# Attention and feed-forward on one core: score matmuls with 128 stationary columns, and reciprocal pieces moved behind each feed-forward step

## The chip, the cores and the metric

The kernel runs on one core of a Trainium2 chip. The metric is the time on the device in microseconds, as a median of several executions; before the change it is 482.2 us (481.5 to 483.6). A trace's span is some 1.8 us shorter than the time of the same execution. All executions told of here were fast ones, with a mean granted TensorE clock of 0.98 or more.

## The reference

```python
q, k, v: (8, 12, 448, 64) fp32;  w_gate, w_val: (768, 1536);  w_out: (1536, 768)
scores = (q @ k.T) / 8                       # per batch and head
attn = exp(scores - max) / (sum(exp(scores - max)) + 1e-9)
x = (attn @ v), heads side by side           # (8*448, 768)
g = x @ w_gate
out = (g * sigmoid(g) * (x @ w_val)) @ w_out # (3584, 768) fp32
```

The kernel leaves the maximum out (the scores are small) and divides by the sum after the product with v.

## The kernel before

Heads go in 48 pairs. For each pair the 448 keys are four chunks of P = 112. A chunk's scores come out keys by queries, so the keys are the stationary operand; the two heads of the pair lie in partitions 0 to 63 and 64 to 127, and their matmuls run side by side in two halves of the array's rows:

```python
def qk_half(pr, half):
    t = qkT[pr]                                    # [128, 2*NC, P]: Q chunks, then K chunks
    for c in (2 * half, 2 * half + 1):
        s = ps_s.tile([P, 2, 512], FP32, tag="s")
        for hx in range(2):
            nc.tensor.matmul(s[:, hx, 0:S],
                lhsT=t[ts(hx, 64), NC + c, :],     # 64 rows, 112 columns
                rhs=t[ts(hx, 64), 0:NC, :].rearrange("p c q -> p (c q)"), ...)
        nc.scalar.activation(E[pr][:, c], s[:, :, 0:S], AF.Exp, scale=sm_scale)
```

Every second pair, the sums of two pairs' exponentials are inverted in four pieces on VectorE, spread over the partitions by four transfers (Rb<-R, below "the broadcast"), and multiplied into X on GpSimd. This work goes into a list, and the feed-forward takes from it:

```python
def sums(p0):
    ...                                            # ssb <- acc, on VectorE
    for i in range(4):
        work.append(lambda i=i: nc.vector.reciprocal(R[:, ts(i, P)], ssb[:, ts(i, P)]))
    def bcast(): ...                               # nc.sync: four transfers R -> Rb
    work.append(bcast)
    return work, [mult(p0), mult(p0 + 1)]          # on GpSimd: X <- xr * Rb

def ffn_run(budget):
    while backlog and budget > 0:
        gen, t = backlog.pop(0)
        pop_deferred(2 if t < 1.5 else 4)          # ahead of the step
        next(gen)                                  # a gp step, a vp step or an op step
        ...
```

A gp step is six matmuls and sg = tanh on ScalarE; a vp step is six matmuls, then t = (sg + 1) * gp and hts = t * vp on VectorE; an op step is twelve matmuls and a copy to osb on ScalarE. gp, vp, op and the sums rotate through three PSUM buffers. osb has two buffers, each freed when its write to the output has landed. SyncE's queue carries, in order, the loads of q and k, the transposing transfers that make qkT from casts done on GpSimd (from pair 11 on, three pairs ahead), the broadcasts and the output writes.

The softmax here doesn't subtract the row's maximum and nothing guards it: scores larger than these inputs give would overflow.

Of the kernel before, what the change touches and what calls it, by code (L numbers as in the profile page):

```python
# [10 lines left out]
FP32 = mybir.dt.float32  # L11
FP16 = mybir.dt.float16
AF = mybir.ActivationFunctionType
# [12 lines left out]
def kernel(  # L26
# [10 lines left out]
    nc = tc.nc  # L37
    B, H, S, D = q.shape
    DM = H * D
    DF = moe_w_gate.shape[1]  # L40
    P = 112
    NC = S // P
# [6 lines left out]
    sm_scale = float(D) ** -0.5  # L49
# [19 lines left out]
    ps_s = ctx.enter_context(tc.tile_pool(name="ps_s", bufs=2, space=PSUM))  # L69
# [6 lines left out]
    ident = consts.tile([P, P], FP16, name="ident")  # L76
# [15 lines left out]
    raw = {}  # L92
    v16 = {}
    qkT = {}
    E = {}
# [48 lines left out]
    def prep(pr):  # L144
        rq, rk = raw[pr]
        if pr == 0 or pr >= NPE:
            qk16 = attp.tile([P, 2, NC, 2, D], FP16, tag="qk16", bufs=3)
            eng = nc.vector if pr == 0 else nc.gpsimd
            for t, src in enumerate((rq, rk)):
                eng.tensor_copy(qk16[:, t].rearrange("p c h d -> p h c d"), src[:])  # L150
        qkT[pr] = attp.tile([128, 2 * NC, P], FP16, tag="qkT", name="qkT", bufs=5)
        if pr >= NPE:
            nc.sync.dma_start_transpose(
                qkT[pr][:], qk16[:].rearrange("p t c h d -> p (t c h d)")
            )
            return None

        def turn():
            tp = ps_f.tile([128, 2 * NC, 128], FP16, tag="f", name="tp")
            for t in range(2):  # L160
                for c in range(NC):
                    for hx in range(2):
                        src = qk16[:, t, c, hx] if pr == 0 else raw[pr][t][:, hx, c, :]
                        nc.tensor.transpose(tp[ts(hx, 64), t * NC + c, 0:P], src, ident[:])  # L164
                if pr == 0 and t == 0:
                    nc.vector.tensor_copy(qkT[pr][:, 0:NC], tp[:, 0:NC, 0:P])
            lo = NC if pr == 0 else 0
            nc.vector.tensor_copy(qkT[pr][:, lo:], tp[:, lo:, 0:P])

        return turn  # L170

    def qk_half(pr, half):
        if half == 0:
            E[pr] = ep.tile([P, NC, 2, S], FP16, tag="E", name="E")
        t = qkT[pr]
        for c in (2 * half, 2 * half + 1):
            s = ps_s.tile([P, 2, 512], FP32, tag="s")
            for hx in range(2):
                nc.tensor.matmul(  # L179
                    s[:, hx, 0:S],  # L180
                    lhsT=t[ts(hx, 64), NC + c, :],
                    rhs=t[ts(hx, 64), 0:NC, :].rearrange("p c q -> p (c q)"),
                    start=True,
                    stop=True,
                )
            nc.scalar.activation(E[pr][:, c], s[:, :, 0:S], AF.Exp, scale=sm_scale)  # L186

    def pv(pr):
        g, r = divmod(pr, GP)
# [15 lines left out]
    def mult(pr, eng, rb, lo=0, hi=S):  # L205
        b, hp = divmod(pr, NHP)
        kk, bb = divmod(b, NB)
        if kk not in X:
            X[kk] = xp.tile([128, NCB, NB * S], FP16, tag="X", name="X")
        eng.tensor_tensor(  # L210
            X[kk][:, hp, bb * S + lo : bb * S + hi], xraw[pr][:, lo:hi], rb[:, lo:hi], ALU.mult
        )

    def sum_rows(p0, acc):
        for c in range(NC):
            for j in range(4):
                nc.tensor.matmul(  # L217
                    acc[ts(j, 32), 0:S],
                    lhsT=ones[:],
                    rhs=E[p0 + j // 2][:, c, j % 2, :],  # L220
                    start=(c == 0),
                    stop=(c == NC - 1),
                )
# [19 lines left out]
    def sums(p0):  # L243
        acc = ps_f.tile([128, 512], FP32, tag="f")
        sum_rows(p0, acc)
        ssb = attp.tile([128, S], FP32, tag="ssb", bufs=1)
        nc.vector.tensor_copy(ssb[:], acc[:, 0:S])  # L247
        R = attp.tile([128, S], FP32, tag="R", bufs=2)
        work = []
        for i in range(4):  # L250
            work.append(lambda i=i: nc.vector.reciprocal(R[:, ts(i, P)], ssb[:, ts(i, P)]))  # L251

        def bcast():
            for u in range(2):
                rb = attp.tile([128, S], FP32, tag="Rb", name="Rb")
                rv = rb[:].rearrange("(r two) s -> two r s", two=2)
                for w in range(2):
                    nc.sync.dma_start(rv[w], R[ts(u, 64), :])
                Rb[p0 + u] = rb

        work.append(bcast)
        return work, [lambda u=u: mult(p0 + u, nc.gpsimd, Rb[p0 + u]) for u in range(2)]

# [80 lines left out]
    with tc.manual_schedule():  # L344
# [17 lines left out]
        for _ in range(7):  # L362
            nc.tensor.matmul(wp[:], lhsT=warm[:, 0:128], rhs=warm[:], start=True, stop=True)
        prep(0)()
        turn = prep(1)

        wq = {
# [18 lines left out]
        deferred = []  # L386
# [5 lines left out]
        def pop_deferred(n=1):  # L392
            for _ in range(n):
                if deferred:
                    deferred.pop(0)()

        def add_block(i):
            f1, f2, n = block(i)
            t1, t2 = NCB * n / 2400.0, NFB * OH / 2400.0
            a = [(f1, t1)] * (2 * NFB)  # L400
            pend = list(ffn2_wait)
            ffn2_wait.clear()
            seq = []
            m = len(pend)
            done = 0
            for x in range(len(a)):
                seq.append(a[x])
                want = (x + 1) * m // len(a)
                while done < want:
                    seq.append(pend[done])  # L410
                    done += 1
            seq += pend[done:]
            own = [(f2, t2)] * (2 * (n // 128))
            if i == 0:
                seq += own
            else:
                ffn2_wait.extend(own)
            backlog.extend(seq)
            state["left"] += sum(t for _, t in seq)

        def ffn_run(budget):
            while backlog and budget > 0:
                gen, t = backlog.pop(0)
                pop_deferred(2 if t < 1.5 else 4)
                next(gen)
                budget -= t
                state["left"] -= t
            return budget

        carry = 0.0  # L430
# [4 lines left out]
        for pr in range(NPAIR + 1):  # L435
            if pr in add_at:
                pop_deferred(99)
# [8 lines left out]
            if pr < NPAIR:  # L446
                qk_half(pr, 0)
            if pr == 0:
                turn()
            if pr + 3 < NPAIR and pr + 3 >= NPE:  # L450
                prep(pr + 3)
# [7 lines left out]
            if pr > NHP and pr % 2 == 0:  # L459
                work, mults = sums(pr - 2)  # L460
                deferred.extend(work)
                held[pr + 1] = mults
            if pr in add_at:
                add_block(add_at[pr])
            for w in wq.pop(pr, []):
                emit(w)
            carry = ffn_run(state["left"] / slots + carry)
            if pr < NPAIR:
                qk_half(pr, 1)
# [8 lines left out]
            if not backlog:  # L478
                pop_deferred(7)
            carry = ffn_run(state["left"] / max(1, slots - 1) + carry)  # L480
        for fns in held.values():
            deferred.extend(fns)
        ffn_run(1e9)
        pop_deferred(99)
        add_block(B - 1)
# [33 lines left out]
```

## Time and profile before

| | before |
|---|---|
| time, median | 482.2 us |
| TensorE busy | 465.8 of 480.3 us |
| first gp step starts | at 40.0 us |
| first gp to the start of the last matmul | 435.9 us |
| TensorE waits for t in that stretch, between starts | 7, sum 5.8 us |

The first 40 us (warm-up, first loads, attention only) differ between executions, and TensorE runs its first matmuls at half clock for a varying time. What sets that is left open. So I compare, besides times, the stretch from the first gp to the start of the last matmul, and give TensorE's losses between starts: the distance of two starts less the streaming time, less 2.5 ns, and less 95 ns where the tiling changes.

The lines below, from the timeline before, give the first group of sums (start, duration, engine, line, operation):

```profile
50.03 2.99 DVE L251 RECIPROCAL R<-ssb 128x112 f32<-128x112 f32 x4
52.93 0.49 DVE L288 SCALAR_TENSOR_TENSOR t<-sg,gp 128x384 f32<-128x384 f32 x1
53.04 2.46 SPq L258 DMA_DIRECT2D Rb<-R  x4
53.48 1.14 PE L268 MATMUL gp<-X,wg 128*128 128x384 f16 x6 [1.08 <-DVE t L288]
```

Four pieces run together, t stands behind them, the next gp waits for t's buffer; and the broadcast leaves at 53.04.

### The profile page before, as it was taken

How to read it: one execution, taken by the hardware profiler on the slowest of the kernel's cores; microseconds unless marked ns; L12 is line 12 of the kernel's file. 1: busy time of each engine (PE TensorE's matmuls, PEld its weight loads, DVE VectorE, ACT ScalarE, POOL GpSimd, SP SyncE). 2: the span in 40 equal slices, each digit the busy share in tenths (PEclk: the TensorE clock that was granted, in tenths of full speed). 3: DMA queues.
4: the chain of work that ended last, by engine and by line, in shares of the span. 5: the costliest groups of instructions: out<-in, count | busy, mean ns of one | idle time of the engine just before them, and what ended most of it. 6: DMA issues, size and time to landing. Idle time of an engine off the chain costs nothing.

```text
span 480.3 us, 8813 instructions
## 1 busy us (share of the span) xinstructions
PE 465.8 (97%) x3559; PEld 226.1 (47%) x3559; DVE 242.1 (50%) x383; ACT 237.5 (49%) x345; POOL 120.7 (25%) x164
## 2 busy tenths in 40 slices
PE   8989999999999999999999999999999999999996
PEld 3435444434444555444444554444444445554553
DVE  3676775167764644636635536446365446343310
ACT  4765555655555455454555465454545551222221
POOL 8534023533243034024042140330320111000000
PEclk9999999999999999999999999999999999999999
DMA  9999999995784596636667476945532212101123
GB/s 138 195 209 239 196 226 182 273 202 125 125 172 97 130 178 140 148 83 162 123 122 179 98 135 131 190 106 129 121 77 65 59 40 72 51 16 33 34 66 100
DMA packets 86025, 62.03 MB, mean 129 GB/s; under 512 B 38496, under 2 KB 82528, under 8 KB 85984
## 3 DMA queue, kind: packets, MB, share of 16 engines
q1 hardware_dynamic: 63872, 46.53, 42.2%
q0 software_dynamic: 22048, 14.88, 22.6%
q8 instruction: 28, 0.46, 0.4%
q14 instruction: 13, 0.11, 0.1%
q10 hardware_dynamic: 64, 0.05, 0.0%
HBM read 47.19 MB, written 11.01 MB: 121 GB/s over the span
## 4 chain that ended last, share of the span: by engine, by line
PE 90%; DVE 6%; ACT 2%; DMA 1%; issue 0%; SPq 0%; ACTq 0%
PE op L304 23%; PE vp L280 22%; PE gp L268 21%; PE s L179 10%; PE acc L194 8%; DVE R L251 4%; PE acc L217 4%; ACT E L186 2%; PE tp L164 1%; PE rb L236 1%; DVE ssb L247 1%; DMA rk<-in_k_dram 1%; DVE t L288 1%; DMA out_dram<-osb 0%; ACT osb L319 0%
## 5 line engine op out<-in xcount | busy, mean ns | idle before, releaser
L186 ACT ACTIVATE E<-s 112x896 f16<-112x896 f32 x192 | 164.5, 915 | 34.0 <-PE s L179 33.9
L268 PE MATMUL gp<-X,wg 128*128 128x384 f16 (+1 forms) x576 | 125.1, 353 | 1.1 <-DVE t L288 1.1
L280 PE MATMUL vp<-X,wv 128*128 128x384 f16 (+1 forms) x576 | 124.9, 353 | 0.5 <-DVE t L288 0.5
L304 PE MATMUL op<-wo,hts 128*128 128x384 f16 x672 | 117.0, 326 | 3.4 <-DVE t L288 3.4
L210 POOL TENSOR_TENSOR X<-xr,Rb 128x448 f16<-128x448 f32 x42 | 47.5, 1133 | 264.6 <-DMA Rb<-R 182.7
L276 ACT ACTIVATE sg<-gp 128x384 f32<-128x384 f32 (+1 forms) x96 | 52.3, 545 | 105.7 <-PE gp L268 105.7
L288 DVE SCALAR_TENSOR_TENSOR t<-sg,gp 128x384 f32<-128x384 f32 (+1 forms) x96 | 58.3, 607 | 79.4 <-ACT sg L276 79.4
L304 PEld LDWEIGHTS <-hts 128*128 128x128 f16 x672 | 64.9, 98 | 51.9 <-issue 8.3
L268 PEld LDWEIGHTS <-wg 128*128 128x128 f16 x576 | 52.6, 98 | 60.8 <-issue 17.3
L280 PEld LDWEIGHTS <-wv 128*128 128x128 f16 x576 | 54.3, 98 | 57.2 <-issue 9.1
L202 DVE COPY xr<-acc 128x448 f32<-128x448 f32 x48 | 29.9, 623 | 92.0 <-PE acc L194 92.0
L291 DVE SCALAR_TENSOR_TENSOR hts<-t,vp 128x384 f16<-128x384 f32 (+1 forms) x96 | 59.6, 621 | 32.2 <-PE vp L280 24.8
L319 ACT ACTIVATE osb<-op 128x384 f32<-128x384 f32 x55 | 27.0, 490 | 97.2 <-PE op L304 93.0
L251 DVE RECIPROCAL R<-ssb 128x112 f32<-128x112 f32 x84 | 62.9, 810 | 0.7
L179 PE MATMUL s<-qkT 64*112 64x448 f16 x384 | 58.9, 378 | 3.8 <-ACT E L186 3.2
L194 PE MATMUL acc<-E,vt 112*32 112x448 f16 x768 | 45.9, 360 | 0.0
L179 PEld LDWEIGHTS <-qkT 64*112 64x112 f16 x384 | 18.6, 126 | 39.2 <-issue 36.3
L194 PEld LDWEIGHTS <-vt 112*32 112x32 f16 x768 | 16.2, 96 | 24.6 <-issue 16.8
L150 POOL CAST qk<-rk 112x512 f16<-112x512 f32 x37 | 22.7, 614 | 0.0
L150 POOL CAST qk<-rq 112x512 f16<-112x512 f32 x37 | 22.7, 613 | 0.0
L217 PE MATMUL acc<-E,ones 112*32 112x448 f16 x384 | 22.3, 353 | 0.0
L126 POOL DMA_DIRECT2D vt<-in_v_dram x17 | 13.5, 792 | 2.7 <-PE acc L194 2.4
(37 smaller groups left out, 94.6 us busy)
## 6 DMA issues: line engine op xcount, KB each, us to landing
Rb<-R SPq DMA_DIRECT2D x84, 112.0 KB, 2.3
rq<-in_q_dram SPq DMA_DIRECT2D x38, 224.0 KB, 3.8
rk<-in_k_dram SPq DMA_DIRECT2D x38, 224.0 KB, 4.0
vt<-in_v_dram POOLq DMA_DIRECT2D x15, 336.0 KB, 6.3
out_dram<-osb SPq DMA_DIRECT2D x7, 336.0 KB, 3.1
wg<-in_moe_w_gate_dram POOLq DMA_DIRECT2D x4, 576.0 KB, 17.8
wv<-in_moe_w_val_dram POOLq DMA_DIRECT2D x4, 576.0 KB, 19.6
wo<-in_moe_w_out_dram POOLq DMA_DIRECT2D x3, 768.0 KB, 28.5
```

Source lines behind the costliest of these rows:

```text
L150: eng.tensor_copy(qk16[:, t].rearrange("p c h d -> p h c d"), src[:])
L179: nc.tensor.matmul(s[:, hx, 0:S], lhsT=t[ts(hx, 64), NC + c, :], rhs=t[ts(hx, 64), 0:NC, :].rearrange("p c q -> p (c q)"), start=True, sto ...
L186: nc.scalar.activation(E[pr][:, c], s[:, :, 0:S], AF.Exp, scale=sm_scale)
L194: nc.tensor.matmul(acc[ts(j, 32), 0:S], lhsT=vt[:, 2 * r + j // 2, c, ts(j % 2, 32)], rhs=E[pr][:, c, j // 2, :], start=(c == 0), stop=(c ...
L210: eng.tensor_tensor(X[kk][:, hp, bb * S + lo : bb * S + hi], xraw[pr][:, lo:hi], rb[:, lo:hi], ALU.mult)
L251: work.append(lambda i=i: nc.vector.reciprocal(R[:, ts(i, P)], ssb[:, ts(i, P)]))
L268: nc.tensor.matmul(gp[:, 0:n], lhsT=wslice("g", fb, cb), rhs=X[kk][:, cb, ds(c0, n)], start=(cb == 0), stop=(cb == NCB - 1),)
L276: nc.scalar.activation(sg[:, 0:n], gp[:, 0:n], AF.Tanh, scale=0.5)
L280: nc.tensor.matmul(vp[:, 0:n], lhsT=wslice("v", fb, cb), rhs=X[kk][:, cb, ds(c0, n)], start=(cb == 0), stop=(cb == NCB - 1),)
L288: nc.vector.scalar_tensor_tensor(t1[:, 0:n], sg[:, 0:n], 1.0, gp[:, 0:n], ALU.add, ALU.mult)
L291: nc.vector.scalar_tensor_tensor(hts[:, fb, 0:n], t1[:, 0:n], 0.5 * HS, vp[:, 0:n], ALU.mult, ALU.mult)
L304: nc.tensor.matmul(op[:, 0:OH], lhsT=hts[:, fb, ts(ch, 128)], rhs=wo[fb // (NFB // 3)][:, fb % (NFB // 3), ts(oh, OH)], start=(fb == 0), s ...
```

## The change

The intent: give the score matmuls the full 128 stationary columns (the 16 beyond the chunk make rows of PSUM that nobody reads), and keep the reciprocals from standing in a row ahead of the feed-forward's own VectorE work.

```diff
-            s = ps_s.tile([P, 2, 512], FP32, tag="s")
+            s = ps_s.tile([128, 2, 512], FP32, tag="s")
...
-                    lhsT=t[ts(hx, 64), NC + c, :],
-                    rhs=t[ts(hx, 64), 0:NC, :].rearrange("p c q -> p (c q)"),
+                    lhsT=t[ts(hx, 64)].rearrange("p c q -> p (c q)")[:, c * P : c * P + 128],
+                    rhs=t[ts(hx, 64), NC:, :].rearrange("p c q -> p (c q)"),
...
-            nc.scalar.activation(E[pr][:, c], s[:, :, 0:S], AF.Exp, scale=sm_scale)
+            nc.scalar.activation(E[pr][:, c], s[0:P, :, 0:S], AF.Exp, scale=sm_scale)
...
+        bcast.light = True
         work.append(bcast)
...
             for _ in range(n):
                 if deferred:
                     deferred.pop(0)()
+                while deferred and getattr(deferred[0], "light", False):
+                    deferred.pop(0)()
...
-                pop_deferred(2 if t < 1.5 else 4)
                 next(gen)
                 budget -= t
                 state["left"] -= t
+                pop_deferred(1 if t < 1.5 else 2)
```

(Cut: the places that fill qkT are changed so that the K chunks come first; the last chunk's 16 extra columns then lie within the tile.)

More of the change, by code (lines that the diff above doesn't have):

```diff
@@ L149, in prep @@
             for t, src in enumerate((rq, rk)):
-                eng.tensor_copy(qk16[:, t].rearrange("p c h d -> p h c d"), src[:])
+                eng.tensor_copy(qk16[:, 1 - t].rearrange("p c h d -> p h c d"), src[:])
         qkT[pr] = attp.tile([128, 2 * NC, P], FP16, tag="qkT", name="qkT", bufs=5)
@@ L162, in turn @@
                     for hx in range(2):
-                        src = qk16[:, t, c, hx] if pr == 0 else raw[pr][t][:, hx, c, :]
-                        nc.tensor.transpose(tp[ts(hx, 64), t * NC + c, 0:P], src, ident[:])
+                        src = qk16[:, 1 - t, c, hx] if pr == 0 else raw[pr][t][:, hx, c, :]
+                        nc.tensor.transpose(tp[ts(hx, 64), (1 - t) * NC + c, 0:P], src, ident[:])
                 if pr == 0 and t == 0:
-                    nc.vector.tensor_copy(qkT[pr][:, 0:NC], tp[:, 0:NC, 0:P])
-            lo = NC if pr == 0 else 0
-            nc.vector.tensor_copy(qkT[pr][:, lo:], tp[:, lo:, 0:P])
+                    nc.vector.tensor_copy(qkT[pr][:, NC:], tp[:, NC:, 0:P])
+            hi = NC if pr == 0 else 2 * NC
+            nc.vector.tensor_copy(qkT[pr][:, 0:hi], tp[:, 0:hi, 0:P])
         return turn
```

## The prediction

> **What bounds the kernel now.** I read the page's busy shares first, then the chain that ended last, then the list of waits, then single stretches of the timeline. The page says:
>
> ```profile
> PE 465.8 (97%) x3559; PEld 226.1 (47%) x3559; DVE 242.1 (50%) x383; ACT 237.5 (49%) x345; POOL 120.7 (25%) x164
> ...
> PE 90%; DVE 6%; ACT 2%; DMA 1%; issue 0%; SPq 0%; ACTq 0%
> ```
>
> TensorE is the bound: 97% busy, 90% of the chain. The chain gives VectorE 6%, 4.4% of it (21 us) to the reciprocal line. That is not a possible gain: a chain walks back through whatever ran, and TensorE was mostly working meanwhile. What a VectorE change can give back is only what TensorE lost, so I take the list of waits, its TensorE rows alone:
>
> ```profile
> PE op L304 <- DVE t L288: 3.4, 5, 1.1
> ...
> PE s L179 <- ACT E L186: 3.2, 7, 0.9
> ...
> PE gp L268 <- DVE t L288: 1.1, 1, 1.1
> ...
> PE vp L280 <- DVE t L288: 0.5, 1, 0.5
> ```
>
> (Columns: microseconds in all, how often, the longest.) Seven waits, 5.0 us, are for the first VectorE instruction of a feed-forward step (t). The timeline shows where one comes from:
>
> ```profile
> 367.32 2.99 DVE L251 RECIPROCAL R<-ssb 128x112 f32<-128x112 f32 x4
> ...
> 367.73 0.49 ACT L276 ACTIVATE sg<-gp 128x384 f32<-128x384 f32 x1 [1.12 <-PE gp L268]
> ...
> 369.12 1.15 PE L268 MATMUL gp<-X,wg 128*128 128x384 f16 x6
> ...
> 370.23 0.49 DVE L288 SCALAR_TENSOR_TENSOR t<-sg,gp 128x384 f32<-128x384 f32 x1
> ...
> 370.78 2.11 PE L304 MATMUL op<-wo,hts 128*128 128x384 f16 x12 [0.51 <-DVE t L288]
> ```
>
> sg is ready at 368.2, but four reciprocal pieces stand ahead of t in VectorE's order and hold it from about 368.2 to 370.2. The feed-forward rotates through three PSUM buffers; gp and vp of this step and gp of the next hold them, so op stands until t has read the first gp.
>
> **The cost of a score set.** Scores come in sets of four matmuls, two row halves side by side, then two more. I looked at one set, and at the gp group that follows it:
>
> ```profile
> L179 PEld LDWEIGHTS <-qkT x4: 123/124/126, 189.8 to 189.8; 64*112 64x112 f16 x4
> L179 PE MATMUL s<-qkT x4: 349/371/393, 189.8 to 190.0; 64*112 64x448 f16 x4
> ```
>
> ```profile
> L268 PEld LDWEIGHTS <-wg x6: 95/98/98, 190.3 to 191.0; 128*128 128x128 f16 x6
> L268 PE MATMUL gp<-X,wg x6: 326/326/336, 190.3 to 191.1; 128*128 128x384 f16 x6
> ```
>
> (Durations are minimum/median/maximum in ns.) After a change of shape the weights cannot be loaded ahead: the first load and the first matmul start within 2 ns of each other in the records (189.827 and 189.829), so the matmul includes the load. For 112 columns that costs 393 - 349 = 44 ns over the second pair, whose load was hidden; for 128 full columns (gp) only 336 - 326 = 10 ns. The start distance confirms it: first to second pair 233 ns (189.829 to 190.062), against 448/2.4 = 187.
>
> **What the Trainium skill says.** "TensorE: Matmul & The Clock Gate", section "Weight-path perf modes — Fast Weight Load (FWL) and DoubleRow": the fast load is on when the number of weights is 128 and the type is not FP32. The trace agrees: loads of 128 columns have a median of 98 ns, those of 112 columns 123. "TensorEngine Tiling (Array Packing)", section "Restrictions", says that column tiling disables the fast load; row tiling, which the scores use, is not named. No run so far shows a 64-row load of 128 columns. The same page's "Key Properties" says that a change of tiling mode drains TensorE: here each switch costs about 95 ns (vp to s 256 ns between starts, against 160 of streaming; s to gp 282 against 187). The change leaves every switch. "Perfetto Trace Analysis", section "Summary: the profiler window per engine type", says that a matmul's end is estimated; so I count losses between starts.
>
> **The change part by part.** *Stationary columns 112 to 128.* Matmul count, moving columns (448) and exponentials are the same; sixteen more PSUM rows are written and not read, and TensorE's time goes by moving columns. K is put ahead of Q in the tile only so that the last chunk's 16 extra columns lie within it; both were needed by the first matmul anyway. The saving is 44 - 10 = 34 ns for each of 384/4 = 96 sets, 3.3 us. Some 8 sets in the first 40 us wait for ScalarE's exponentials, so there it is hidden: 88 x 34 = 3.0 us. If the two row halves load one after the other, the second adds another 10 ns: 88 x 24 = 2.1 us. I take 2.7.
>
> *Reciprocals.* The same 84 pieces, about 747 ns each (2.99/4), same VectorE sum. In the new instruction order the typical run is: one piece, t and hts, one or two pieces, t and hts, and the last one, in place of four ahead of t. For the stretch above: ssb copied at 367.3, one piece until 368.1, t from 368.2 (ready sg) to 368.7, hts when vp ends, then the rest. The first gp is free at 368.7 and op wants it at 370.1: 1.4 us to spare. Two pieces together (1.5 us) may delay the next t, but a wait of 0.5 to 1.1 us after four pieces means that with 1.5 us less nothing is left. Counted between starts, the seven losses beyond streaming and a switch's 95 ns are 1.15 (at 53.5 us), 0.67 (69.9), 0.68 (146.1), 0.69 (258.5), 0.68 (370.8), 0.67 (386.2), 1.30 (401.1): 5.8 us. It is more than 5.0 because the modelled matmul tail, 326 - 162 = 164 ns, hides part of a gap. After 40 us I find no other gap above 60 ns that is not a switch, so nothing stands behind these seven: 5.8 us come off.
>
> *The broadcast and the X products move later.* The broadcast now follows its last piece at once, but that piece lies 1 to 2 steps later; the products come out of the list one at a time. By the sum of streaming times in program order they move 1 to 3 us. The last product before a block's first gp ends, before and in order of blocks, 1.5, 6.2, 9.5, 10.1, 7.2, 8.4 and 10.3 us ahead of it (for the first: product done 94.3, gp 95.8). The tight first one lies in a stretch of op steps where VectorE has no feed-forward work, so its four pieces still run together and its broadcast keeps its place in the DMA queue. No wait should arise.
>
> Sum: 5.8 + 2.7 = 8.5 us; 482.0 - 8.5 = 473.5 us.
>
> **Rivals.** *The fast load doesn't engage with 64 rows.* Then the load grows by 16 columns, about 7 ns at one column per 2.4 GHz cycle (an estimate), 96 x 7 = 0.7 us lost, and 482.0 - 5.8 + 0.7 = 476.9. For it: no load of this form is in the trace; against: the rule as stated has no row condition. I give it one in six. *The products become the wait.* If the broadcasts stall the SP queue or products land late, blocks start late by 1 to 2 us each: 475 to 480. For it: the 1.5 us margin; against: the other margins of over 6 us. *VectorE as the new bound.* It is half busy, with runs of reciprocals moved rather than added; if half the seven waits came back elsewhere, 476.4. *The chain taken at its word:* 21 us of reciprocals would make 461; the TensorE waits speak against it.
>
> **Range and chances.** The reciprocal part is nearly sure, the weight part likely. Everything at its best (44 ns x 96 = 4.2 us, and 5.8) gives 472.0, just beyond the 2% line at 472.3. So the likely result is just within 2%. I say 473.5 us, 471.5 to 477.0; faster by over 2% 0.15, within 2% 0.83, slower 0.02.
>
> **What would show it.** Right: score loads near 98 ns and the first matmul of a set near 360 ns in place of 393; the three TensorE rows that wait for t gone; the gain of the weights spread evenly over 0 to 392 us, that of the reciprocals in steps at the seven places. Wrong: score loads at 123 ns or above; a TensorE wait for X; new waits for t after two or three pieces in a row. Most dangerous to the number is what I have not seen in the trace at all, the speed of the 64-row fast load.

## The result

The changed kernel takes 474.6 us (474.1 to 475.1, four executions), against 482.2 us. The ratio is 0.984, interval 0.981 to 0.987. The time lies in the range forecast, 1.1 us above the figure in it.

The page of the changed kernel, busy shares and chain:

```profile
PE 461.7 (98%) x3559; PEld 219.4 (46%) x3559; DVE 245.3 (52%) x383; ACT 237.4 (50%) x345; POOL 120.8 (26%) x164
...
PE 91%; ACT 3%; DMA 3%; issue 1%; SPq 0%; DVE 0%; POOL 0%; ACTq 0%; POOLq 0%
```

VectorE has gone from the chain (6% to 0%), yet the time fell by 1.6%: its share in the chain was no measure of the gain. DMA went from 1% to 3% and ScalarE from 2% to 3%.

The list of waits after. No TensorE row waits for t any more; these have grown or are new:

```profile
PE s L179 <- ACT E L186: 4.4, 10, 0.9
...
ACT osb L320 <- DMA out_dram<-osb: 3.0, 1, 3.0
...
PEld L179 <- DMA qkT<-qk: 0.9, 1, 0.9
```

Before, the first was 3.2 us in 7 waits, the second 1.5 us, and the third did not exist.

The score line by itself, over the whole trace after (minimum/median/maximum in ns):

```profile
L179 PEld LDWEIGHTS <-qkT x384: 92/93/115, 6.1 to 385.9; 64*128 64x128 f16 x192
L179 PE MATMUL s<-qkT x384: 346/359/578, 6.1 to 386.1; 64*128 64x448 f16 x192
```

The load fell from 123 to 93 ns, the first matmul of a set from 393 to 359; the second pair has a median of 349 in both traces.

The stretch of the timeline that answers to the one in the prediction (the same step, 4.2 us earlier):

```profile
363.11 0.85 DVE L251 RECIPROCAL R<-ssb 128x112 f32<-128x112 f32 x1
...
363.52 0.49 ACT L277 ACTIVATE sg<-gp 128x384 f32<-128x384 f32 x1 [1.09 <-PE gp L269]
364.04 0.56 DVE L289 SCALAR_TENSOR_TENSOR t<-sg,gp 128x384 f32<-128x384 f32 x1
...
365.18 2.27 DVE L251 RECIPROCAL R<-ssb 128x112 f32<-128x112 f32 x3
365.86 1.30 PE L305 MATMUL op<-wo,hts 128*128 128x384 f16 x7
```

One piece, then t as soon as sg is there, and op starts with no wait; three pieces run after hts, where nobody needs VectorE.

Between 74 and 94 us, though, TensorE now waits where it did not. The timeline there:

```profile
59.44 8.26 SPq L153 DMA_TRANSPOSE qkT<-qk  x1
...
70.31 4.16 SPq L153 DMA_TRANSPOSE qkT<-qk  x1
...
74.56 2.46 SPq L258 DMA_DIRECT2D Rb<-R  x4
...
76.75 0.11 PEld L179 LDWEIGHTS <-qkT 64*128 64x128 f16 x4 [0.90 <-DMA qkT<-qk]
76.76 0.55 PE L179 MATMUL s<-qkT 64*128 64x448 f16 x4 [0.52 <-ACT osb L320]
...
90.67 0.49 ACT L320 ACTIVATE osb<-op 128x384 f32<-128x384 f32 x1 [3.05 <-DMA out_dram<-osb]
91.06 1.72 ACT L186 ACTIVATE E<-s 112x896 f16<-112x896 f32 x2
...
92.02 0.36 PE L179 MATMUL s<-qkT 64*128 64x448 f16 x2 [0.58 <-ACT E L186]
...
92.83 0.37 PE L179 MATMUL s<-qkT 64*128 64x448 f16 x2 [0.44 <-ACT E L186]
```

At 76.76 the first score set of pair 12 starts late; its weight load had waited for that pair's transposed keys. Their transfer was the one issued from 59.44 to 67.70, and by its semaphore it landed at 76.71; the transfer issued at 70.31 carries pair 13. (The matmul's own label names osb only because that copy ended at the same moment.) At 90.67 ScalarE's copy to osb waits for an output write to free a buffer, the exponentials stand behind it, and two more score pairs wait for them. Between starts these three cost 0.59, 0.65 and 0.62 us, 1.86 us in all.

From the first gp to the last matmul the changed kernel takes 429.4 us, 6.4 less than before: 5.8 from the waits for t, less 1.9 of new waits, which leaves 2.5 for the weight loads.

### The profile page after: what moved, and what is told of

Read it like the earlier page. It is cut to its first block, busy times and chain, and to the rows that moved or that the text cites. A ratio compares the mean times of both kernels' runs of the same rounds, so it can differ in the third digit from the quotient of the medians.

```text
span 473.3 us, 8811 instructions
## 1 busy us (share of the span) xinstructions
PE 461.7 (98%) x3559; PEld 219.4 (46%) x3559; DVE 245.3 (52%) x383; ACT 237.4 (50%) x345; POOL 120.8 (26%) x164
## 4 chain that ended last, share of the span: by engine, by line
PE 91%; ACT 3%; DMA 3%; issue 1%; SPq 0%; DVE 0%; POOL 0%; ACTq 0%; POOLq 0%
PE gp L269 24%; PE vp L281 24%; PE op L305 21%; PE s L179 9%; PE acc L194 8%; PE acc L217 4%; ACT E L186 3%; PE rb L236 1%; DMA out_dram<-osb 1%; PE tp L164 1%; DMA Rb<-R 1%; DMA rk<-in_k_dram 1%; SPq L153 0%; POOL qk L150 0%; POOL X L210 0%
## 5 line engine op out<-in xcount | busy, mean ns | idle before, releaser
L251 DVE RECIPROCAL R<-ssb 128x112 f32<-128x112 f32 x84 | 66.9, 828 | 0.7
L179 PE MATMUL s<-qkT 64*128 64x448 f16 x384 | 55.6, 361 | 5.6 <-ACT E L186 4.4
L179 PEld LDWEIGHTS <-qkT 64*128 64x128 f16 x384 | 12.3, 94 | 41.4 <-issue 37.8
```

The costliest lines, as they stand in the source:

```text
L179: nc.tensor.matmul(s[:, hx, 0:S], lhsT=t[ts(hx, 64)].rearrange("p c q -> p (c q)")[:, c * P : c * P + 128], rhs=t[ts(hx, 64), NC:, :].rear ...
```

## The experiments

Twelve more runs were made, on three chips (stat_only to early_old; osb3 to behind2; after_again to behind2_osb3), each with the kernel before beside it (medians 482.2, 482.3 and 482.2 us). All gave correct results; one, after_again, is the changed kernel once more. The first builds of osb3, prep4 and osb3_prep4 did not fit into SBUF; in those that ran, and in behind2_osb3, t is written over sg to make room, and a control run (inplace) has that alone.

| kernel | time, median (range), us | ratio to before, interval | first gp to last matmul, us | TensorE losses in it, us |
|---|---|---|---|---|
| before | 482.2 | | 435.9 | t: 5.8 |
| changed | 474.6 (474.1 to 475.1) | 0.984, 0.981 to 0.987 | 429.4 | 77 to 93 us: 1.9 |
| stat_only | 479.6 (479.2 to 480.3) | 0.995, 0.993 to 0.996 | 433.5 | t: 6.0 |
| recip_only | 477.2 (476.5 to 477.4) | 0.990, 0.988 to 0.991 | 430.1 | none |
| cols120 | 476.9 (476.9 to 479.0) | 0.990, 0.988 to 0.992 | 431.2 | 91 to 92 us: 0.9 |
| early_old | 475.0 (474.5 to 475.5) | 0.985, 0.983 to 0.986 | 429.4 | t: 1.9 |
| osb3 | 472.9 (472.3 to 473.7) | 0.981, 0.979 to 0.983 | 427.8 | 75 us: 0.2 |
| prep4 | 481.7 (478.6 to 484.2) | 0.998, 0.995 to 1.002 | 436.2 | 77 to 103 us, large |
| osb3_prep4 | 479.7 (475.4 to 480.8) | 0.993, 0.990 to 0.996 | 433.9 | 97 to 103 us, large |
| behind2 | 472.9 (472.8 to 473.8) | 0.981, 0.979 to 0.983 | 428.0 | 53 us: 0.4 |
| after_again | 475.7 (474.3 to 477.3) | 0.985, 0.983 to 0.987 | 430.9 | 79 to 95 us: 3.4 |
| inplace | 475.5 (472.6 to 476.3) | 0.985, 0.983 to 0.988 | 429.5 | 78 to 93 us: 1.9 |
| late_piece | 474.5 (473.8 to 476.3) | 0.985, 0.982 to 0.987 | 429.7 | 77 to 93 us: 2.1 |
| behind2_osb3 | 474.2 (473.6 to 474.7) | 0.983, 0.981 to 0.985 | 428.0 | 55 us: 0.4 |

The two last columns are of the one execution that left a trace, so a comparison of them is of one execution with one.

**stat_only: the stationary columns alone.**

```diff
 (the changed kernel with the list of work taken as before)
+                pop_deferred(2 if t < 1.5 else 4)
                 next(gen)
-                pop_deferred(1 if t < 1.5 else 2)
```

> Only the 128 stationary columns; the reciprocals as before. Theory A (the load of 128 columns is fast and takes 33 ns off the first matmul of each score set): 88 x 33 ns = 2.9 us, so about 479.3 us, ratio 0.994; score loads near 93 ns, first matmul of a set near 360 ns; the seven waits for t stay, 5.8 us between starts; no new waits at 77 and 92 us, since the early stalls still hold TensorE back. Rival (the gain comes from elsewhere, the loads were hidden): within 0.5 us of before.

Measured 479.6 us, 2.5 under before. Loads have a median of 94 ns, the second pair of a set starts 200 ns after the first in place of 233, the seven waits for t are all there, and no others. The fast load is real and is worth 2.5 us; the rival falls.

**recip_only: the reciprocal order alone** (the kernel before, with the two hunks about the list of work).

> Only the reciprocal order; 112 stationary columns. The seven waits for t go (5.8 us between starts). Theory D (the new waits near 77 and 92 us are transfers that land at a fixed time, which an earlier TensorE merely runs into): TensorE gets there with less of a lead than in the full change, so the new waits sum to about 0.8 us and the time is about 477.2 us. Rival O (the moved broadcasts and products cause the waits): they sum to the same 1.85 us as in the full change, and the time is about 478.2 us.

Measured 477.2 us, 5.0 under before, as theory D said. But the trace does not bear out its reason: it is of the fastest execution (476.5) and has no wait at all after 40 us. The other three executions were 0.6 to 0.9 us slower and left no trace; whether they had the waits is not shown. With the same order of work the new waits can be absent, then, and this run does not decide between D and O. The gains of the two parts, 2.5 and 5.0, add up to that of the whole, 7.6.

**cols120: neither 112 nor 128 columns.**

```diff
-            s = ps_s.tile([128, 2, 512], FP32, tag="s")
+            s = ps_s.tile([120, 2, 512], FP32, tag="s")
-    ...[:, c * P : c * P + 128],
+    ...[:, c * P : c * P + 120],
```

> The full change with 120 stationary columns in place of 128. If the fast load needs exactly 128: loads of 123 ns or a little more, first matmul of a set near 396 ns, and about 3 us over the full change, so near 477.6 us. If the gain came from the order of K and Q in the tile, or from a gradual effect of the number of columns: near 474.6 us.

The score line of its trace:

```profile
L179 PEld LDWEIGHTS <-qkT x384: 126/126/221, 6.2 to 387.7; 64*120 64x120 f16 x192
L179 PE MATMUL s<-qkT x384: 346/397/626, 6.2 to 387.9; 64*120 64x448 f16 x192
```

At 120 columns the first matmul is 4 ns slower than at 112 (397 against 393), at 128 it is 34 ns faster. It is a step at the full 128, not a slope, and neither the order of K and Q nor a wider output makes it. The time of 476.9 us lies within the noise of the 477.6 expected.

**early_old: the old order of reciprocals until pair 12.**

```diff
-                pop_deferred(1 if t < 1.5 else 2)
+                (before next(gen), while pr < 12)  pop_deferred(2 if t < 1.5 else 4)
+                (from pr = 12 on, after it)        pop_deferred(1 if t < 1.5 else 2)
```

> The full change, but until pair 12 the reciprocals are taken as before (several, ahead of the step); from pair 12 on as in the change. The two early stalls (1.15 us at 53 us, 0.67 us at 70 us) come back. Theory D: the waits at 77 and 92 us go, since TensorE no longer has the lead, and the time is that of the full change within 0.4 us (474.6). Rival (the waits at 77 and 92 us have another cause, the wider score matmuls or the output buffers alone): they stay, and the time is 1.8 us longer, 476.4.

Both early stalls are back (1.18 and 0.71 us), the waits between 74 and 94 us are gone, and the stretch from the first gp is 429.4 us, the same as in the changed kernel. In the changed kernel's traced execution, then, taking away the two early stalls brought nothing: what TensorE won there it gave back 7 to 40 us later. Both D and O fit this.

**osb3, prep4, osb3_prep4: loosening what TensorE waits for.** A third staging buffer, casts and transposing transfers a pair earlier, and both.

```diff
-            osb = fp.tile([128, DM], FP32, tag="osb", bufs=2)
+            osb = fp.tile([128, DM], FP32, tag="osb", bufs=3)     # osb3, osb3_prep4
-            if pr + 3 < NPAIR and pr + 3 >= NPE:
-                prep(pr + 3)
+            if pr + 4 < NPAIR and pr + 4 >= NPE:                  # prep4, osb3_prep4
+                prep(pr + 4)                                      # and qkT with bufs=6
```

> The full change with three output staging buffers in place of two (t is written over sg to make room). Theory D (in the stretch of 40 to 95 us the time is set by transfers that land late: the transposed keys at 77 us, the output write that frees a staging buffer at 92 us): the two waits at 92 us (0.65 and 0.6 us) go, the one at 77 us stays when it occurs; about 473.9 us against 474.6. Rival M (the stretch is bound by the transfers as a whole, and the next one takes the place): nothing gained, 474.6, with a new wait at the first gp of block 1 or at a score set.

> The full change with the casts and the transposing transfers issued four pairs ahead in place of three (t written over sg to make room). Theory D: the wait at 77 us (0.6 us) goes, those at 92 us stay; about 474.2 us. Rival M: nothing gained, 474.6.

> Both of them together. Theory D: no TensorE wait beyond a switch after 40 us; the time is what the prediction had without new waits, 473.4 us, 1.2 us under the full change. Rival M: 474.6, with the waits elsewhere in the stretch.

osb3 is as D expected, and more: 472.9 us, no wait at 92 us, 0.2 us at 75 us. prep4 missed everything: 481.7 us, all of the gain lost. Its list of waits shows why:

```profile
ACT osb L320 <- DMA out_dram<-osb: 6.5, 1, 6.5
PE s L179 <- DMA Rb<-R: 4.1, 1, 4.1
...
PE op L305 <- DMA wo<-in_moe_w_out_dram: 1.4, 1, 1.4
```

Counted from the first gp, the last two loads of wo leave as early as in the changed kernel (0.7 and 4.7 us, against 0.6 and 4.8) but land 3.3 to 3.7 us later, and op waits 1.4 us for one of them. The third transposing transfer holds SyncE's queue for 11.3 us, and what stands behind it comes later too: the second broadcast leaves at 38.7 us after the first gp, against 35.2. That the earlier transposing transfers slowed the loads is likely, but no run shows it. The label of the wait of 4.1 us names a broadcast; the exponential that the score set needed had ended just before it (96.84 us), behind the copy to osb that had waited 6.5 us. After this wait TensorE ran at half clock: the granted clock was 0.53 from 97 to 103 us. osb3_prep4 does not wait for osb, but for X (3.2 us in two waits), and had a granted clock of 0.50 in the same stretch. Rival M, "the stretch is bound by the transfers as a whole", fits prep4: starting this one kind of transfer earlier moved the wait elsewhere. It is wrong about osb3.

**behind2: two pieces behind each step.**

```diff
-                pop_deferred(1 if t < 1.5 else 2)
+                pop_deferred(2 if t < 1.5 else 4)
```

> The full change, but two pieces (four after an op step) behind each step in place of one (two). If the place behind the step is what counts: no wait for t, as in the full change, 474.6 us. If the number per step counts: two pieces after gp and two more after vp stand between t and hts as before or ahead of the next t; two pieces are 1.5 us, less than the 3 us of before, so waits for t of 0.3 us at most each and under 1 us in all, 475.5 us at most.

Measured 472.9 us, 1.7 under the changed kernel of another call, which neither theory had. No wait for t came back, and the waits between 74 and 94 us are absent. One gp loses 0.4 us at 53 us: it waits for a VectorE copy of transposed keys, which stood behind two pieces. The first group of sums in its timeline:

```profile
48.63 1.57 DVE L251 RECIPROCAL R<-ssb 128x112 f32<-128x112 f32 x2
50.11 0.49 DVE L289 SCALAR_TENSOR_TENSOR t<-sg,gp 128x384 f32<-128x384 f32 x1
...
51.18 1.56 DVE L251 RECIPROCAL R<-ssb 128x112 f32<-128x112 f32 x2
52.76 2.46 SPq L258 DMA_DIRECT2D Rb<-R  x4
```

and in the changed kernel:

```profile
51.79 0.84 DVE L251 RECIPROCAL R<-ssb 128x112 f32<-128x112 f32 x1
53.03 0.84 DVE L251 RECIPROCAL R<-ssb 128x112 f32<-128x112 f32 x1
...
54.86 0.85 DVE L251 RECIPROCAL R<-ssb 128x112 f32<-128x112 f32 x1
55.73 1.82 SPq L258 DMA_DIRECT2D Rb<-R  x3
```

The broadcast can leave only when the fourth piece is done. It leaves 14.1 us after the first gp in behind2, 16.4 us in the changed kernel, 13.0 us before. That would fit theory O, and the last four runs were to test it.

**late_piece: behind2 with the fourth piece alone one step later.**

```diff
         for i in range(4):
+            if i == 3:
+                work.extend([lambda: None] * 3)
             work.append(lambda i=i: nc.vector.reciprocal(...))
```

> behind2 with only the fourth reciprocal piece held back by one feed-forward step, to where the change has it; the order of the transfers in their queue is that of behind2 and of the change. Theory O (the broadcast waits for the fourth piece, and a later first broadcast delays the X products, the casts, the transposed keys and the output writes behind them, until TensorE meets them at 70 to 95 us): first broadcast 17 us after the first gp in place of 15, waits of 0.5 to 1.9 us in that stretch, 474.3 us. Theory N (behind2 is faster for another reason, such as the order of products, or by luck of the execution): 472.9 us without waits there.

(The 17 and 15 us, and the 17.5 below, were reckoned from a first gp 1.2 us too early; on the scale used here they are 16 and 14.) The waits are back: 0.65, 0.81 and 0.62 us, at 77, 93 and 93 us, with the broadcast 15.9 us after the first gp, and the median is 474.5 us. The page of waits has the same three rows as that of the changed kernel, the transposed keys 1.0 us, the output write 3.2, the exponentials 4.3. In the kernel nothing else differs from behind2; the order in SyncE's queue is the same. This is what theory O expected. It does not rule out N, the luck of the execution: behind2 ran in another call, each kernel has one trace, and late_piece's five executions (473.8 to 476.3 us) overlap with those of behind2_osb3 in its own call (473.6 to 474.7).

**after_again and inplace: the changed kernel once more, and the control for osb3.**

> The changed kernel once more, beside the others of this call. 474.6 us; executions differ by about 1 us. In its trace the waits between 70 and 95 us sum to 0.5 to 1.9 us, and the first broadcast of R is issued some 17.5 us after the first gp.

> Control for osb3: the full change with t written over sg, and the two staging buffers of the change. If the gain of osb3 came from the third buffer: 474.6 us. If it came from writing t in place: 472.9 us.

after_again: 475.7 us, executions from 474.3 to 477.3. Its trace is of the slowest one, and has the same three waits, longer: 1.86, 0.88 and 0.62 us, 3.4 in all, above the 1.9 expected at most. inplace has them with 0.92, 0.40 and 0.62 us. The waits at 93 us are there with two buffers and gone with three, so the third buffer takes them away; what that gains in time is compared across two calls. One of inplace's six executions took 472.6 us; I read it as one without the waits, which no trace shows.

**behind2_osb3: both remedies.**

```diff
-                pop_deferred(1 if t < 1.5 else 2)
+                pop_deferred(2 if t < 1.5 else 4)
-            osb = fp.tile([128, DM], FP32, tag="osb", bufs=2)
+            osb = fp.tile([128, DM], FP32, tag="osb", bufs=3)
```

> Two pieces behind each step and three staging buffers. Both theories: no wait beyond a switch after 60 us. If the two remedies work on the same waits, as theory O has it: no faster than either alone by more than 0.4 us, 472.6 us. If they add: 471.2 us.

From the first gp it takes 428.0 us, exactly as behind2 alone and 2.9 less than after_again: the remedies work on the same waits and do not add. Its median of 474.2 us is above the 472.9 of either alone; its trace starts the feed-forward at 40.0 us in place of 38.7 (behind2), so I put the difference to the start, not to the remedies. The steps after the first gp are what the experiments can compare; the start alone can move a time by more than 1 us.

**How the wait travels.** In the changed kernel's trace the links can be followed. The first broadcast is issued at 55.73, among the loads of weights, q, k and v. The transposing transfer of pair 12 stands directly behind it and two loads in SyncE's queue; it lands at 76.71, which is the wait at 77 us. The broadcast's data come for the first X product at 65.52 and for the second at 67.97. The casts stand behind those products on GpSimd and run from 69.05 to 71.3; the transposing transfer of pair 13 follows and holds SyncE's queue to 74.5; the second broadcast leaves only then, at 74.56, and has landed at 80.7. The next products, casts, transposes and the output writes behind them follow in the same way, until a write issued at 84.80 lets the copy to osb go at 90.67, which makes the two waits at 92 us.

**What stays open.** That the later first broadcast is what makes these transfers late (theory O) is not shown. In the trace before, with its early broadcast, they were as late. These are the transfer of pair 12, the longest time from issue to landing of a transposing transfer between 40 and 96 us, and the copy to osb:

```profile
57.86 11.51 SPq L153 DMA_TRANSPOSE qkT<-qk  x1
...
DMA to landing us min/median/max: 3.6/7.1/20.1
...
91.32 0.49 ACT L319 ACTIVATE osb<-op 128x384 f32<-128x384 f32 x1 [1.48 <-DMA out_dram<-osb]
```

Counted from the first gp, pair 12's keys landed at 37.9 us before and at 37.3 in the changed kernel, the second broadcast left at 35.5 and 35.2, the write that frees osb landed at 51.2 and 51.1. In the trace before, TensorE reached pair 12 only at 38.9 us, because the two early stalls had held it back by 1.8. Without stalls it is ready for that set at 36.8 us, and the wait at 77 us is what the landing exceeds that by. The landing varies: 36.0 to 37.9 us in the five traces with a broadcast at 13 to 14 us, 35.0 to 38.6 in the seven with one at 16 us and no casts moved (35.0 is recip_only). The early broadcasts land earlier on the whole, but the groups overlap. So the comparison of before and after fits D (the transfers land late, and an earlier TensorE runs into them), that of behind2 and late_piece fits O, and with one trace for each kernel the two are not told apart. What is shown is that removing the stalls brings TensorE to transfers that had no slack.

## Why the prediction was right or wrong

*The bound and the seven waits.* Right that all seven would go, 5.8 us between starts; "so nothing stands behind these seven: 5.8 us come off" failed for the two early ones, 1.8 us, as the next step but one tells; two or three pieces in a row, after hts, cost TensorE nothing in the changed kernel.

*The fast load.* Right. It engages for 64 rows, loads are at 93 ns, the first matmul of a set at 359, the predicted 360. The gain per set was put at 24 to 34 ns; it came out at 2.5 us over the 81 sets after the first gp (the prediction counted 88), 31 ns each. stat_only alone gives 2.5, against 2.7.

*"The broadcast and the X products move later ... No wait should arise."* This is the step that failed, and with it "nothing stands behind these seven". The shift itself was foreseen at 1 to 3 us, and measured 3.3 us for the first broadcast. But I held it only against the last product before each block's first gp. The products wait for the broadcast on GpSimd, the casts stand behind the products, the transposes behind the casts, and the output writes behind those on SyncE. That chain had no margin even before: the copy to osb at 91.32 of that trace waits 1.48 us for its write, and pair 12's keys landed 1.0 us ahead of a TensorE that had been held back by 1.8. The cost was three waits, 1.9 us, in the traced execution; other traces with the late broadcast have between none and 3.4. Whether the shift or only TensorE's earlier arrival brings the waits stays open, as told above.

*The rivals.* The second, "if the broadcasts stall the SP queue", is what happened in part, with 0.2 to 3.4 us in place of 1 to 2 us for each block, and at score sets rather than at the blocks' start. The later blocks show none of it: all the waits of the changed kernel lie before 96 us. The other rivals, no fast load and VectorE as a new bound, did not come.

*The sum.* 5.8 + 2.5 - 1.9 = 6.4 us from the first gp on, against 8.5 forecast. The changed kernel's first gp also came 0.6 us earlier in its trace, which nothing in the change was forecast to do, and the medians are 7.6 us apart. So the 473.5 us were missed by only 1.1 us in part by luck; the failed step alone made 1.9. The traces of behind2 and osb3 have most of that back, with 472.9 us each. Their intervals (0.979 to 0.983) overlap slightly with that of the changed kernel (0.981 to 0.987), so the claim that they beat it rests on the traces as much as on the times.

## What to carry to other kernels

A VectorE instruction that was moved out of the way of one consumer may have another, behind a transfer: follow each moved result to its last reader, through every in-order queue it passes, and not only to the next matmul. Take the gain of a removed wait from the waits of the bounding engine, measured between starts, and not from the chain's shares; then ask what the engine will meet when it comes earlier, for an old stall can hide a wait behind it. Where a stationary operand is a little short of 128 columns of a 16-bit type and its load stands behind a change of tiling, try widening it to 128: here that took 31 ns off each set.

## What the Trainium skill lacked or had wrong

- "TensorE: Matmul & The Clock Gate", section "Weight-path perf modes — Fast Weight Load (FWL) and DoubleRow", gives the condition of 128 weights, and the runs agree with it as a sharp step: first matmul of a set 393 ns at 112 columns, 397 at 120, 359 at 128. The page's section "LDWEIGHTS (loading the stationary operand)" says that a load of fewer rows takes the same time, and here 64 rows by 128 columns load in 93 ns, against 98 for 128 rows. That the fast load works with row tiling is said nowhere in so many words; "TensorEngine Tiling (Array Packing)", section "Restrictions", speaks of column tiling alone.
- "TensorEngine Tiling (Array Packing)", section "Key Properties", says that a change of mode drains TensorE and gives no duration; here it is about 95 ns between starts.
- "TensorE: Matmul & The Clock Gate", section "HAM oscillation — how this bites in real kernels", warns of gaps of over about 3.4 us. prep4 agrees: after a wait of 4.1 us the granted clock was 0.53 for 6 us. In osb3_prep4 two waits of 3.2 us together, the longer 2.7, were followed by 0.50 in the same way, so a single gap of that length was not needed here.
- "DMA: Bandwidth & Descriptors", section "DMA Transpose (X-bar)", gives no time for which a transposing transfer holds the queue that issues it; here that took 1.2 us at the least, and 8.3 us (changed) and 11.5 us (before) while weights were loading.
